# Holding the normalising products of four head pairs back by one pair, and running their reciprocals in one go

## The chip, the cores and the metric

The kernel runs on one NeuronCore of a Trainium2 chip. A core has five engines with a queue of instructions each: TensorE (PE, matmuls; its weight loads are listed apart as PEld), VectorE (DVE), ScalarE (ACT), GpSimd (POOL) and SyncE (SP, which here only issues transfers). Each queue is worked off in its order; an instruction that waits for another engine or for a transfer holds up all that stands behind it in its own queue. Transfers run on 16 DMA engines. The metric is the device time of the launch in microseconds (us); the median of three runs before the change is 471.52 us (471.06 to 471.65).

## The reference

Softmax attention, and on its output a gated feed-forward block (SwiGLU):

```python
# q, k, v: (8, 12, 448, 64)
scores = q @ k.transpose(0, 1, 3, 2) / sqrt(64)
attn = exp(scores - max(scores)); attn = attn / sum(attn)
x = (attn @ v).transpose(0, 2, 1, 3).reshape(3584, 768)
g = x @ w_gate                     # (768, 1536)
out = (silu(g) * (x @ w_val)) @ w_out   # (1536, 768)
```

## The kernel before, in words

**Pairs.** The 96 heads are worked off as 48 pairs; six pairs make a batch of 448 rows, and one X tile holds two batches: pairs 0 to 11 fill the first one. The main loop (L475) has one iteration `pr` for each pair, in which stages of several pairs lie beside one another:

- `load_qk16` (L118) fetches q and k of two pairs ahead, cast to fp16, from POOL's queue; `load_v` (L127) does so for v.
- `prep(pr + 3)` (L497): from pair 11 on, POOL copies q and k into one tile (L156, the two COPY qk<-q and qk<-k), and SP issues a transposing transfer of it (L159). There are three such tiles.
- `qk_half` (L179) makes scores on PE (L186) and their exponentials E on ACT (L193).
- `pv(pr - 1)` (L195): 16 matmuls into the one PSUM bank `acc` (L201), which VectorE copies out to `xr` (L209). There are four xr tiles.
- every other iteration `sums(pr - 2)` (L270) for two pairs: row sums on PE (L224), a copy (`ssb`), and then pieces of work that are put on a list: four reciprocals on VectorE (L278, 112 columns each), and four transfers from SP that spread the result R over partitions as Rb (L285).
- `mult` (L212, L217) multiplies xr by Rb into X on POOL, one instruction for each pair, from pair 6 on. It frees the xr tile and completes X.

**The feed-forward block** is cut in eight blocks of 384 or 512 rows, worked in small steps between the attention stages: gate products (gp) and a tanh on ACT, value products (vp) and two products on VectorE (`ffn1_steps`, L303), then the output products (op), a copy on ACT and the stores from SP (`ffn2_steps`, L335). Block 0 needs pairs 0 to 5 and is added at iteration 6. Block 1 needs pairs 6 to 11 as well and is added at iteration 15; the later ones follow at 21, 27 and so on. The steps of block 0 end with its six output steps, which fall in iterations 11 to 14.

**The order** is written out by hand: each engine gets its instructions as the Python program emits them. Reciprocals, spreading transfers and products are not emitted at once. `sums` puts the four reciprocals and the transfers on the list `deferred`; the products go into `held`, under the iteration at whose end they are moved to `deferred` (L518, L543). `ffn_run` (L461) emits feed-forward steps and after each takes work off `deferred` (L467): one piece after a short step, two after an output step, and the transfers at once when they come to the front. When a block is added, everything deferred is emitted first (L477).

So the iteration under which products are held decides what stands before them in POOL's queue, and the number taken off at a time decides where the reciprocals stand among VectorE's instructions and the transfers among SP's.

Of the kernel before, what the change touches and what calls it, by code (L numbers as in the profile page):

```python
# [27 lines left out]
def kernel(  # L28
# [77 lines left out]
    def dummy(n):  # L106
        wp = ps_f.tile([128, 512], FP32, tag="f", name="wp")
        for _ in range(n):
            nc.tensor.matmul(wp[:], lhsT=warm[:, 0:128], rhs=warm[:], start=True, stop=True)

    def load_qk0():
        rq = raws.tile([P, 2, NC, D], FP32, tag="rq", bufs=RB)
        rk = raws.tile([P, 2, NC, D], FP32, tag="rk", bufs=RB)
        for dst, src in ((rq, q), (rk, k)):
            nc.sync.dma_start(dst[:], src[0, 0:2].rearrange("h (p c) d -> p h (c d)", c=NC))
        raw[0] = (rq[:], rk[:])

    def load_qk16(pr, n=2):  # L118
        q16 = raws.tile([P, 4, NC, D], FP16, tag="rq", bufs=RB, name="q16")
        k16 = raws.tile([P, 4, NC, D], FP16, tag="rk", bufs=RB, name="k16")  # L120
        for dst, src in ((q16, q), (k16, k)):
            flat = src.rearrange("b h s d -> (b h) s d")[2 * pr : 2 * pr + 2 * n]
            nc.gpsimd.dma_start(dst[:, 0 : 2 * n], flat.rearrange("h (p c) d -> p h (c d)", c=NC))
        for i in range(n):
            raw[pr + i] = (q16[:, 2 * i : 2 * i + 2], k16[:, 2 * i : 2 * i + 2])

    def load_v(g, lo=0, hi=2 * GP):  # L127
        b = g // GPB
        h0 = (g % GPB) * 2 * GP
        if lo == 0:  # L130
            v16[g] = raws.tile([P, 2 * GP, NC, D], FP16, tag="vt", bufs=3, name="vt")
        nc.gpsimd.dma_start(
            v16[g][:, lo:hi],
            v[b, h0 + lo : h0 + hi].rearrange("h (p c) d -> p h (c d)", c=NC),
        )
# [247 lines left out]
    with tc.manual_schedule():  # L383
        load_qk0()
        nc.vector.memset(warm[:], 0.0)
        nc.vector.memset(ones[:], 1.0)
        nc.vector.memset(sel[:], 0.0)
        for u in range(2):
            for hx in range(2):
                r = 64 * u + 32 * hx  # L390
                nc.vector.memset(sel[r : r + 1, u, ts(hx, 64)], 1.0)
        load_qk16(1, 1)
        make_identity(nc, ident)
        load_v(0, 0, 2)
        load_qk16(2, 1)
        load_v(0, 2)
        load_qk16(3, 1)
        load_qk16(4)
        load_v(1)
        dummy(7)  # L400
        prep(0)()
        dummy(1)
        turn = prep(1)

        wq = {
            0: [("qk", 6), ("g", 0, 0), ("v", 0, 0)],
            1: [("V", 2), ("qk", 8), ("g", 1, 0), ("v", 1, 0)],
            3: [("g", 2, 0), ("v", 2, 0)],
            4: [("qk", 10), ("g", 2, NCB // 2), ("v", 2, NCB // 2)],
            5: [("V", 3)],  # L410
            6: [("o", 0, 0)],
            7: [("o", 1, 0)],
            8: [("o", 2, 0)],
        }

        def emit(item):
            if item[0] == "qk":
                load_qk16(*item[1:])
            elif item[0] == "V":
                load_v(item[1])  # L420
            else:
                load_w(*item)

        deferred = []
        held = {}
        backlog = []
        state = {"left": 0.0}
        ffn2_wait = []

        def pop_deferred(n=1):  # L430
            for _ in range(n):
                if deferred:
                    deferred.pop(0)()
                while deferred and getattr(deferred[0], "light", False):
                    deferred.pop(0)()

        def add_block(i):
            f1, f2, n = block(i)
            t1, t2 = NCB * n / 2400.0, NFB * OH / 2400.0
            a = [(f1, t1)] * (2 * NFB)  # L440
            pend = list(ffn2_wait)
            ffn2_wait.clear()
            seq = []
            m = len(pend)
            done = 0
            for x in range(len(a)):
                seq.append(a[x])
                want = (x + 1) * m // len(a)
                while done < want:
                    seq.append(pend[done])  # L450
                    done += 1
            seq += pend[done:]
            own = [(f2, t2)] * (2 * (n // 128))
            if i == 0:
                seq += own
            else:
                ffn2_wait.extend(own)
            backlog.extend(seq)
            state["left"] += sum(t for _, t in seq)

        def ffn_run(budget):  # L461
            while backlog and budget > 0:
                gen, t = backlog.pop(0)
                next(gen)
                budget -= t
                state["left"] -= t
                pop_deferred(1 if t < 1.5 else 2)  # L467
            return budget

        carry = 0.0  # L470
        DELAY = 3
        add_at = {FIRST: 0}
        for i in range(1, B - 1):
            add_at[NHP * (i + 1) + DELAY] = i
        for pr in range(NPAIR + 1):  # L475
            if pr in add_at:
                pop_deferred(99)  # L477
            nxt = min([x for x in add_at if x > pr] + [NPAIR + 4])
            slots = 2 * (nxt - pr)
            turn2 = None  # L480
            if pr % 2 == 0 and 12 <= pr + LA < NPAIR:
                load_qk16(pr + LA)
            if pr == NHP:
                pv(pr - 1)
                acc5 = sums64(pr - 1)
                rb4 = scale64(pr - 2, acc4)
                rb5 = scale64(pr - 1, acc5)
                load_table("exp_and_others")
                mult(pr - 2, nc.vector, rb4)
            if pr < NPAIR:  # L490
                qk_half(pr, 0)
            if pr == 0:
                dummy(1)
                turn()
                dummy(1)
            if pr + 3 < NPAIR and pr + 3 >= NPE:
                prep(pr + 3)  # L497
            if pr + 2 < NPAIR:
                if pr + 2 < NPE:
                    turn2 = prep(pr + 2)  # L500
                if (pr + 2) % GP == GP - 1 and 4 <= (pr + 2) // GP + 1 < NGRP:
                    load_v((pr + 2) // GP + 1)
            if pr >= 1 and pr != NHP:
                pv(pr - 1)
            if pr == 5:
                spread23((0,))
            if pr in (2, 4):
                spread = sums_pe(pr - 2, ((0, S),))
            if pr == NHP:
                spread23((1,))  # L510
                mult(pr - 1, nc.vector, rb5)
                dummy(6)
                add_block(0)
                ffn_run(2.5)
            if pr > NHP and pr % 2 == 0:
                work, mults = sums(pr - 2)
                deferred.extend(work)
                held[pr + 1] = mults  # L518
            if pr in add_at and pr != FIRST:
                add_block(add_at[pr])  # L520
            for w in wq.pop(pr, []):
                emit(w)
            tiled[0] = pr >= TILED
            if pr != FIRST:
                carry = ffn_run(state["left"] / slots + carry)
            tiled[0] = False
            if pr < NPAIR:
                qk_half(pr, 1)
            if pr == 0:
                dummy(2)  # L530
            if turn2:
                turn2()
            if pr in (3, 4):
                spread01((pr - 3,))
            if pr == 5:
                acc4 = sums64(pr - 1)
            if pr == 2:
                spread01 = spread
            if pr == 4:
                spread23 = spread  # L540
            if pr == FIRST:
                slots -= 1
            for fn in held.pop(pr, []):  # L543
                deferred.append(fn)
            if not backlog:
                pop_deferred(7)
            carry = ffn_run(state["left"] / max(1, slots - 1) + carry)
        for fns in held.values():
            deferred.extend(fns)
        ffn_run(1e9)  # L550
        pop_deferred(99)
        add_block(B - 1)
        ffn_run(1e9)
        backlog.extend(ffn2_wait)
        ffn_run(1e9)
# [30 lines left out]
```

The softmax here doesn't subtract the row's maximum and nothing guards it: scores larger than these inputs give would overflow.

## Time and profile before

| What | Value |
|---|---|
| time, median of 3 | 471.52 us |
| span of the profiled execution | 470.7 us |
| PE busy | 459.2 us (98%) |
| ACT, DVE, POOL busy | 240.8, 240.7, 146.5 us |
| POOL waiting for Rb (pairs 6 to 47) | 209.2 us in 30 waits |
| PE waiting for X | 3.6 us in 2 waits |
| products of pairs 8 and 9 start | 77.7 and 80.1 us |
| products of pairs 10 and 11 start | 94.65 and 95.7 us |
| block 1's first gate product starts | 91.84 us |
| row sums of pairs 10 and 11 start | 74.63 us |

A timeline row gives the start from the beginning of the span, the length, the engine and line, the operation with the tile written and the tiles read, how many instructions were merged in the row, and in brackets the idle time before it with what ended it. A row of waits gives the total, the number and the longest. A row of windows gives, for a stretch of time, the busy time of PE, PEld, DVE, ACT and POOL, and then PE's granted clock, the DMA share and GB/s.

### The profile page before, as it was taken

The page shows a single profiled execution, that of the slowest core. Times are in us where ns is not written, and L with a number is a line of the kernel's source. Part 1 is how long each engine was busy: PE and PEld are TensorE (multiplying, and loading weights), DVE is VectorE, ACT ScalarE, POOL GpSimd, SP SyncE. Part 2 cuts the span into 40 slices and gives each one's busy share as a digit, 9 for nine tenths or more (in the row PEclk, how much of TensorE's full clock was granted, in tenths as well). Part 3 has the DMA queues.
Part 4 walks back from the last instruction along what each step waited for, and adds up shares of the span by engine and source line. Part 5 has one row for each costly group of instructions (what it writes and reads, how often), then busy time and mean ns, then how long its engine had stood idle before and what let it go on. Part 6 is the DMA issues. An engine that isn't in the chain of part 4 may idle for free.

```text
span 470.7 us, 12521 instructions
## 1 busy us (share of the span) xinstructions
PE 459.2 (98%) x5435; PEld 227.7 (48%) x5435; DVE 240.7 (51%) x375; ACT 240.8 (51%) x350; POOL 146.5 (31%) x200
## 2 busy tenths in 40 slices
PE   8899999879999999999999999999999999999996
PEld 3344444434445555444445555544444555554453
DVE  3665775336764564563654644645636554334310
ACT  4886666636555455455546546546454542222221
POOL 8533352255555225405054054143120011000000
PEclk9999999989999999999999999999999999999999
DMA  9999999999987689647595694884352123201123
GB/s 138 194 203 206 202 191 151 176 167 115 137 138 117 116 138 150 122 50 135 87 142 101 111 154 86 149 105 93 50 115 57 26 68 81 59 1 35 33 68 100
DMA packets 85430, 53.76 MB, mean 114 GB/s; under 512 B 37888, under 2 KB 81920, under 8 KB 85376
## 3 DMA queue, kind: packets, MB, share of 16 engines
q0 software_dynamic: 39200, 23.37, 36.7%
q1 hardware_dynamic: 46112, 29.55, 31.5%
q8 instruction: 42, 0.69, 0.6%
q14 instruction: 12, 0.10, 0.1%
q10 hardware_dynamic: 64, 0.05, 0.0%
HBM read 47.19 MB, written 11.01 MB: 124 GB/s over the span
## 4 chain that ended last, share of the span: by engine, by line
PE 93%; DMA 3%; ACT 1%; POOL 1%; SPq 1%; issue 0%; DVE 0%; POOLq 0%; ACTq 0%
PE op L296 17%; PE vp L296 16%; PE gp L296 12%; PE gp L299 11%; PE s L186 9%; PE vp L299 8%; PE acc L201 8%; PE op L299 5%; PE acc L224 4%; ACT E L193 1%; DMA k<-in_k_dram 1%; DMA Rb<-R 1%; PE rb L263 1%; PE tp L170 1%; SPq L159 0%
## 5 line engine op out<-in xcount | busy, mean ns | idle before, releaser
L193 ACT ACTIVATE E<-s 112x896 f16<-112x896 f32 x192 | 164.6, 915 | 27.6 <-PE s L186 27.5
L217 POOL TENSOR_TENSOR X<-xr,Rb 128x448 f16<-128x448 f32 x42 | 47.7, 1140 | 222.6 <-DMA Rb<-R 209.2
L315 ACT ACTIVATE sg<-gp 128x384 f32<-128x384 f32 (+1 forms) x96 | 52.3, 545 | 100.5 <-PE gp L299 58.5
L327 DVE SCALAR_TENSOR_TENSOR t<-sg,gp 128x384 f32<-128x384 f32 (+1 forms) x96 | 58.8, 612 | 84.7 <-ACT sg L315 84.7
L296 PE MATMUL op<-wo,hts 128*128 128x384 f16 x516 | 89.7, 326 | 0.0
L296 PE MATMUL vp<-X,wv 128*128 128x384 f16 (+1 forms) x378 | 81.6, 352 | 0.0
L330 DVE SCALAR_TENSOR_TENSOR hts<-t,vp 128x384 f16<-128x384 f32 (+1 forms) x96 | 59.6, 621 | 34.2 <-PE vp L296 21.5
L358 ACT ACTIVATE osb<-op 128x384 f32<-128x384 f32 x55 | 27.0, 490 | 95.2 <-PE op L296 67.4
L209 DVE COPY xr<-acc 128x448 f32<-128x448 f32 x48 | 29.8, 621 | 75.6 <-PE acc L201 69.7
L296 PEld LDWEIGHTS <-hts 128*128 128x128 f16 x516 | 49.8, 98 | 37.1 <-issue 2.8
L278 DVE RECIPROCAL R<-ssb 128x112 f32<-128x112 f32 x84 | 66.3, 825 | 0.6
L299 PE MATMUL gp<-X,wg 128*32 128x512 f16 (+1 forms) x1080 | 61.1, 359 | 3.6 <-POOL X L217 3.6
L296 PE MATMUL gp<-X,wg 128*128 128x384 f16 (+1 forms) x306 | 64.6, 348 | 0.0
L186 PE MATMUL s<-qkT 64*128 64x448 f16 x384 | 54.3, 356 | 2.0 <-ACT E L193 1.8
L296 PEld LDWEIGHTS <-wv 128*128 128x128 f16 x378 | 34.9, 98 | 38.1 <-issue 8.2
L201 PE MATMUL acc<-E,vt 112*32 112x448 f16 x768 | 45.2, 355 | 0.0
L299 PE MATMUL vp<-X,wv 128*32 128x512 f16 (+1 forms) x792 | 45.0, 363 | 0.0
L296 PEld LDWEIGHTS <-wg 128*128 128x128 f16 x306 | 28.6, 98 | 28.9 <-issue 6.2
L299 PEld LDWEIGHTS <-wg 128*32 128x32 f16 x1080 | 29.0, 97 | 27.6 <-issue 4.2
L299 PEld LDWEIGHTS <-wv 128*32 128x32 f16 x792 | 21.7, 98 | 17.2 <-issue 0.9
L186 PEld LDWEIGHTS <-qkT 64*128 64x128 f16 x384 | 11.8, 94 | 37.5 <-issue 35.6
L201 PEld LDWEIGHTS <-vt 112*32 112x32 f16 x768 | 16.1, 96 | 25.1 <-issue 16.8
(47 smaller groups left out, 248.0 us busy)
## 6 DMA issues: line engine op xcount, KB each, us to landing
Rb<-R SPq DMA_DIRECT2D x84, 112.0 KB, 2.5
vt<-in_v_dram POOLq DMA_DIRECT2D x15, 336.0 KB, 6.2
q<-in_q_dram POOLq DMA_DIRECT2D x22, 224.0 KB, 4.3
k<-in_k_dram POOLq DMA_DIRECT2D x22, 224.0 KB, 5.7
out_dram<-osb SPq DMA_DIRECT2D x7, 336.0 KB, 3.4
wg<-in_moe_w_gate_dram POOLq DMA_DIRECT2D x4, 576.0 KB, 16.2
wv<-in_moe_w_val_dram POOLq DMA_DIRECT2D x4, 576.0 KB, 17.7
wo<-in_moe_w_out_dram POOLq DMA_DIRECT2D x3, 768.0 KB, 20.0
```

Source lines behind the costliest of these rows:

```text
L186: nc.tensor.matmul(s[:, hx, 0:S], lhsT=t[ts(hx, 64)].rearrange("p c q -> p (c q)")[:, c * P : c * P + 128], rhs=t[ts(hx, 64), NC:, :].rear ...
L193: nc.scalar.activation(E[pr][:, c], s[0:P, :, 0:S], AF.Exp, scale=sm_scale)
L201: nc.tensor.matmul(acc[ts(j, 32), 0:S], lhsT=vt[:, 2 * r + j // 2, c, ts(j % 2, 32)], rhs=E[pr][:, c, j // 2, :], start=(c == 0), stop=(c ...
L209: nc.vector.tensor_copy(xr[:], acc[:, 0:S])
L217: eng.tensor_tensor(X[kk][:, hp, bb * S + lo : bb * S + hi], xraw[pr][:, lo:hi], rb[:, lo:hi], ALU.mult)
L278: work.append(lambda i=i: nc.vector.reciprocal(R[:, ts(i, P)], ssb[:, ts(i, P)]))
L296: nc.tensor.matmul(dst, lhsT=lhsT, rhs=rhs, start=start, stop=stop)
L299: nc.tensor.matmul(dst[ts(j, 32), :], lhsT=lhsT[:, ts(j, 32)], rhs=rhs, start=start, stop=stop)
L315: nc.scalar.activation(sg[:, 0:n], gp[:, 0:n], AF.Tanh, scale=0.5)
L327: nc.vector.scalar_tensor_tensor(t1[:, 0:n], sg[:, 0:n], 1.0, gp[:, 0:n], ALU.add, ALU.mult)
L330: nc.vector.scalar_tensor_tensor(hts[:, fb, 0:n], t1[:, 0:n], 0.5 * HS, vp[:, 0:n], ALU.mult, ALU.mult)
L358: nc.scalar.activation(osb[:, ts(oh, OH)], op[:, 0:OH], AF.Copy, scale=1.0 / HS)
```

## The change

The products of pairs 8 to 11 are held one iteration longer (those of 8 and 9 until iteration 12, those of 10 and 11 until 14), so that loads and copies for later pairs stand ahead of them in POOL's queue. Up to iteration 15, four deferred pieces instead of two are taken off after an output step, so that the four reciprocals of pairs 10 and 11 follow one another and their spreading transfers are emitted sooner.

```diff
-        state = {"left": 0.0}
+        state = {"left": 0.0, "many": 4}
...
-                pop_deferred(1 if t < 1.5 else 2)
+                pop_deferred(1 if t < 1.5 else state["many"])
...
                 work, mults = sums(pr - 2)
                 deferred.extend(work)
-                held[pr + 1] = mults
+                held[pr + (2 if pr in (10, 12) else 1)] = mults
             if pr in add_at and pr != FIRST:
+                state["many"] = 2
                 add_block(add_at[pr])
```

In the built program nothing is added or left out. On POOL the two products of pairs 8 and 9 move behind the q and k loads for pair 18, the copies for pairs 15 and 16 and a load of v; those of pairs 10 and 11 move behind the loads for pair 20 and the copies for pair 17. On VectorE the four reciprocals of pairs 10 and 11 come together, ahead of an xr copy. On SP the four spreading transfers of pairs 10 and 11 move ahead of the transpose of pair 16, and those of pairs 12 and 13 ahead of two output stores.

## Prediction

> **What bounds the kernel now.** I read the page's busy shares first, then what the matmul engine (PE) waited for, then the stretch of its timeline where it waited, then the chain that ended last through that stretch, and last the queue of GpSimd (POOL) before it.
>
> The page, busy shares and granted clock:
>
> ```profile
> PE 459.2 (98%) x5435; PEld 227.7 (48%) x5435; DVE 240.7 (51%) x375; ACT 240.8 (51%) x350; POOL 146.5 (31%) x200
> ...
> PEclk9999999989999999999999999999999999999999
> ```
>
> PE is busy for 98% of the span, the others for half or less. So an edit off PE can gain only where PE stands still, or where its clock is cut. One slice of 40 has a lower clock: the ninth, at 94 to 106 us. The table of waits, for PE alone:
>
> ```profile
> PE gp L299 <- POOL X L217: 3.6, 2, 2.9
> PE s L186 <- ACT E L193: 1.8, 5, 0.4
> ```
>
> The only stall of any size is a gate product that waits for X, twice, 3.6 us. PE's timeline there (start, length, idle before):
>
> ```profile
> 91.84 1.04 PE L299 MATMUL gp<-X,wg 128*32 128x512 f16 x16
> 95.83 0.40 PE L299 MATMUL gp<-X,wg 128*32 128x512 f16 x4 [2.95 <-POOL X L217]
> 96.92 0.46 PE L299 MATMUL gp<-X,wg 128*32 128x512 f16 x4 [0.69 <-POOL X L217]
> 97.13 2.81 PE L299 MATMUL vp<-X,wv 128*32 128x512 f16 x24
> 99.87 0.86 PE L186 MATMUL s<-qkT 64*128 64x448 f16 x4
> ...
> 105.36 1.47 PE L299 MATMUL gp<-X,wg 128*32 128x512 f16 x24
> 106.66 1.47 PE L299 MATMUL vp<-X,wv 128*32 128x512 f16 x24
> ```
>
> This is the first gate product of block 1, in iteration 15. Its first 16 matmuls read pairs 6 to 9; the next four need pair 10 and the last four pair 11. After the gap 24 value matmuls take 2.81 us, where the same 24 take 1.47 at 106.66. The clock in that stretch, by windows of 2 us (the third figure from the end is the share of full speed):
>
> ```profile
> 96.00:98.00 2.00, 1.31 (x17) 0.51 (x16) 0.43 (x1) 0.58 (x1) 2.00 (x3) 0.78 0.00 0
> 98.00:100.00 2.00, 2.00 (x22) 0.69 (x16) 0.71 (x2) 0.02 (x1) 2.00 (x5) 0.50 1.02 123
> ```
>
> 0.78, then 0.50. **What the gap is worth:** from 91.84 to the start of the next gate product at 100.66 it is 8.82 us. The same work (24 gp, 24 vp, 4 s) from 105.36 to 108.55 takes 3.19. The difference is 5.63 us: 3.64 idle, and about 2.0 of slow matmuls.
>
> Why X was late, from the chain that ended last:
>
> ```profile
> 86.29 1.86 SPq L159
> ...
> 88.25 1.18 SPq L285
> ...
> 89.48 5.01 DMA Rb<-R
> ...
> 94.65 0.71 POOL X L217
> ...
> 95.74 1.13 POOL X L217
> ```
>
> The reciprocals of pairs 10 and 11 ended at 81.68 (VectorE's timeline: two at 76.28, two at 80.12), yet their spreading transfers (L285) were issued from 88.25, behind a transpose (L159) and two output stores on SyncE's queue. That queue stood from 73.25 to 83.85 on a transpose whose input POOL had not copied. POOL's timeline says why:
>
> ```profile
> 77.72 1.13 POOL L217 TENSOR_TENSOR X<-xr,Rb 128x448 f16<-128x448 f32 x1 [8.73 <-DMA Rb<-R]
> 80.14 1.13 POOL L217 TENSOR_TENSOR X<-xr,Rb 128x448 f16<-128x448 f32 x1 [1.29 <-DMA Rb<-R]
> ...
> 82.65 0.62 POOL L156 COPY qk<-q 112x512 f16<-112x512 f16 x1
> ```
>
> From 68.99 POOL stood at the products of pairs 8 and 9, whose Rb landed late (7.4 to 8.9 us after issue); the copies for pairs 15 and 16 were queued behind them. So POOL's wait held SyncE, SyncE held Rb of pairs 10 and 11, and that held PE.
>
> **What the Trainium skill says.** "TensorE: Matmul & The Clock Gate", Part 1 (The HAM clock gate): about 3.4 us of idleness halves PE's clock, and as much busy time brings it back; its window runs freely, so the size varies from run to run. The trace agrees: 3.64 us idle, then 0.50 of full clock. "DMA: Bandwidth & Descriptors", Anatomy of one DMA: a wait sits on the issuing sequencer, not in the DMA engines, so what is queued behind it is not even issued; the 6.6 us from 81.68 to 88.25 are that. Same page, Queues, rings and completion order: each DMA engine serves a queue's ring in order and alternates between queues by packets; so more loads in flight slow the Rb transfers. The trace agrees in kind: from 72 to 78 both queues carried packets and Rb took 7.4 to 8.9 us to land, against a median of 2.5 for all 84.
>
> **The change part by part.** No instruction is added or taken away; the built order moves some. (1) On POOL the products of pairs 8 and 9 go behind the loads for pair 18, the copies for 15 and 16 and a load of v. Those of 10 and 11 go behind the load for pair 20 and the copies for 17. (2) On VectorE the four reciprocals of pairs 10 and 11 run in one go, ahead of the xr copy of pair 12. (3) On SyncE the Rb issues of 10 and 11 stand ahead of pair 16's transpose, and those of 12 and 13 ahead of a pair of output stores.
>
> (2) costs nothing: they start at 76.28 and take 2.99 (the row of four at 86.88), so end at 79.27; the xr copy behind them waits for PE until 79.46 anyway. R is ready 2.4 us sooner.
>
> (1) POOL after 68.99: two load issues (0.76 + 0.71), copies for 15 (1.1), v issue (0.77): 72.4. Then the copies for pair 16 wait for their own loads: q, issued at 65.27, landed 11.7 later, at 77.0; k, at 66.02, landed 13.9 later, at 79.9. So they end near 80.5. Rb of 8 and 9 are there by then (77.7, 80.1), so the two products end near 82.8. Here is the added wait: the xr copy of pair 12 (four xraw buffers) needs the product of pair 8 done, near 81.7, and ends at 82.3; PE needs its PSUM bank at 84.47 for the next pv. 2.2 us of slack. Load issues for pair 20 and the copies for 17 follow: 82.8 + 1.45 + 1.1 = 85.4.
>
> (3) SyncE: pair 15's transpose no longer waits (issued by 74.6). Two stores wait for ScalarE's osb, which ends at 78.63; out by 79.7. Then the four Rb issues at 0.6 each: 79.7 to 82.2, where before they ran from 88.25 to 92.40. Their landing is the unknown, as the loads for 18 and v are now in flight with them. Bounds: 3.5 us (shortest here) and 8.9 (the longest on this kernel's Rb rows): 85.1 to 90.5 for the last, issued at 81.6. I take 7.6, the median of the loaded stretch: 89.2. Products of 10 and 11 then end by about 90.4, at the upper bound by 91.6 to 92.8. PE needs pair 10 at 92.7 and pair 11 at 92.9. So X is ready just in time even at the bound.
>
> Sum: 5.63 us come off PE, which is the bound from there to the end (every 10-us window looked at after 100 us shows PE busy throughout). 471.52 - 5.63 = 465.89. I keep 0.1 for waits of a few tenths such as those on E: **466.0**.
>
> **Rivals.**
> - A remnant of the gap. Rb lands later than 8.9 us, since stores of 384 KB and a transpose stand ahead of it in its queue; the transposes of that time took up to 13.1 us to land. At 81.6 + 10.5 = 92.1 the last product ends at 93.3 to 94.4: 0.5 to 1.5 us idle, too short for the clock to drop: 466.5 to 467.4. At 13.1 it is about 3 us, with part of the clock loss: 470. Against it: loads are spread over a stretch with room in it (from 80 to 82 us the DMA share was 0).
> - The wait changes places. The product of pair 8 now stands behind the copies of pair 16, which wait for k. If that lands at 22.1 us (the longest q load of that stretch) rather than 13.9, it is 88.1; pair 8's product ends at 89.9, xr of 12 at 90.5, and PE stands from 84.47 to 90.5. 6.0 us idle plus 2.0 of slow clock, against 5.63 gained, and pair 10's products late on top, some 2 us: 471.5 - 5.6 + 8.0 + 2 = 476. Slower. Against: that 22.1 us load shared the queues with three weight loads, all landed by 71.9.
> - Nothing: Rb is as late as before, because the earlier loads only fill the same DMA engines: 471.5. Against: six us earlier issue is more than any spread of landing here.
>
> **How the numbers follow.** Forecast 0.66; remnant 0.20; wait elsewhere, slower 0.10; nothing 0.04. The range takes the forecast with some 0.8 us below (a different clock loss in other runs) and the remnant up to 3 us: 465.2 to 469.0. It leaves out the last two and the worst remnant, under 2 in 10. Faster 0.87 (forecast, remnant, a little of nothing), same 0.03, slower 0.10.
>
> **What would show it.** Right: PE's waits on X gone or under 1 us, no slice with a lower clock after the start, Rb of 10 and 11 issued near 80, pair 15's transpose issued near 74, pair 16's copies waiting for the k load until about 80, products of 8 and 9 near 81 to 83, of 10 and 11 done before 92.5. Wrong: PE waiting on the xr copy's bank near 84, or still on X near 93; or a gap at a later block's start, which nothing before shows.

## The result, and the profile after

The changed kernel takes 467.15 us (466.85 to 468.27, four runs) against 471.58 for the kernel before (471.06 to 474.2, four runs): a ratio of 0.9899, with a 95% interval of 0.9859 to 0.994. Run again later beside 47 runs of the kernel before it took 467.06 (466.57 to 468.04) against 472.04: 0.9898, 0.9879 to 0.9918. So it is faster by 1.0%, some 4.4 to 5.0 us; the forecast was 466.0.

The page of the changed kernel, busy shares and granted clock:

```profile
PE 457.0 (98%) x5435; PEld 227.3 (49%) x5435; DVE 240.6 (52%) x375; ACT 240.7 (52%) x350; POOL 146.5 (32%) x200
...
PEclk9999999999999999999999999999999999999999
```

It is the same work, and the one slice with a lower clock is gone. In the table of what PE waited for, the longest row is now the one that stood second:

```profile
PE s L186 <- ACT E L193: 1.8, 5, 0.4
```

No row with X is left. PE's timeline at the start of block 1:

```profile
91.17 0.94 PE L201 MATMUL acc<-E,vt 112*32 112x448 f16 x16
91.94 1.47 PE L299 MATMUL gp<-X,wg 128*32 128x512 f16 x24
93.24 1.47 PE L299 MATMUL vp<-X,wv 128*32 128x512 f16 x24
94.64 0.55 PE L186 MATMUL s<-qkT 64*128 64x448 f16 x4
95.12 1.47 PE L296 MATMUL gp<-X,wg 128*128 128x512 f16 x6
```

All 24 gate matmuls come in one row. From 91.94 to the next gate product it takes 3.18 us, where the kernel before took 8.82. That next gate product starts 5.54 us sooner than before, and the span is 5.5 us shorter, so in these two executions the whole gain arises here. GpSimd's timeline, with what it waited for in brackets:

```profile
77.37 0.61 POOL L156 COPY qk<-q 112x512 f16<-112x512 f16 x1 [4.68 <-DMA q<-in_q_dram]
80.77 0.61 POOL L156 COPY qk<-k 112x512 f16<-112x512 f16 x1 [2.79 <-DMA k<-in_k_dram]
81.35 2.23 POOL L217 TENSOR_TENSOR X<-xr,Rb 128x448 f16<-128x448 f32 x2
...
88.78 2.22 POOL L217 TENSOR_TENSOR X<-xr,Rb 128x448 f16<-128x448 f32 x2 [2.66 <-DMA Rb<-R]
```

The copies of pair 16 now wait for their own loads ahead of the products of pairs 8 and 9; those of pairs 10 and 11 end at 91.0 instead of 96.9. SyncE's queue in the kernel before, where the row of two transposes stretched to 85 us:

```profile
71.79 13.29 SPq L159 DMA_TRANSPOSE qkT<-qk  x2
...
88.25 4.15 SPq L285 DMA_DIRECT2D Rb<-R  x4
```

and in the changed kernel:

```profile
71.99 6.24 SPq L159 DMA_TRANSPOSE qkT<-qk  x2
...
79.77 2.40 SPq L285 DMA_DIRECT2D Rb<-R  x4
```

The row of transposes now ends at 78.2, and Rb of pairs 10 and 11 is issued 8.5 us sooner. Some 2.6 us of this are lost again, because these four transfers now land 8.1 to 8.5 us after their issue, where it was 3.5 to 5.8 before; the products end 5.9 us sooner. The price is in VectorE's timeline:

```profile
82.52 0.62 DVE L209 COPY xr<-acc 128x448 f32<-128x448 f32 x1 [3.16 <-POOL X L217]
```

The xr copy of pair 12 waits for the product of pair 8. It ends at 83.1, and PE uses the freed bank at 84.57, so this wait is hidden.

### The profile page after: what moved, and what is told of

Read it like the earlier page. It is cut to its first block, busy times and chain, and to the rows that moved or that the text cites. A ratio compares the mean times of both kernels' runs of the same rounds, so it can differ in the third digit from the quotient of the medians.

```text
span 465.2 us, 12522 instructions
## 1 busy us (share of the span) xinstructions
PE 457.0 (98%) x5435; PEld 227.3 (49%) x5435; DVE 240.6 (52%) x375; ACT 240.7 (52%) x350; POOL 146.5 (32%) x200
## 4 chain that ended last, share of the span: by engine, by line
PE 95%; DMA 2%; ACT 1%; POOL 1%; issue 0%; DVE 0%; ACTq 0%; POOLq 0%
PE op L296 18%; PE vp L296 16%; PE gp L296 12%; PE gp L299 11%; PE s L186 9%; PE acc L201 9%; PE vp L299 8%; PE op L299 5%; PE acc L224 4%; ACT E L193 1%; DMA k<-in_k_dram 1%; PE rb L263 1%; PE tp L170 1%; DMA out_dram<-osb 0%; PE acc L236 0%
## 5 line engine op out<-in xcount | busy, mean ns | idle before, releaser
L299 PE MATMUL vp<-X,wv 128*32 128x512 f16 (+1 forms) x792 | 43.7, 355 | 0.0
```

The lines of the kernel that those rows point to most:

```text
L299: nc.tensor.matmul(dst[ts(j, 32), :], lhsT=lhsT[:, ts(j, 32)], rhs=rhs, start=start, stop=stop)
```

## Experiments

The theory was a chain of queues: GpSimd's wait for Rb of pairs 8 and 9 held the copies of pair 15, these held SyncE's queue, that held Rb of pairs 10 and 11, and that PE. The rivals were that the reciprocals alone were late, or that transfers were slow wherever they stood. In some runs of the kernel before PE's clock was cut and in others it was not, so the mean granted clock of each run is used beside its time. The runs with the hold alone, the reciprocals alone, the filled gap and the changed kernel ran on one chip, beside 47 runs of the kernel before (median 472.04); the second profile of the hold alone and the last three experiments ran on another, beside 30 (median 471.56).

**The longer hold alone** (against the changed kernel):

```diff
-        state = {"left": 0.0, "many": 4}
+        state = {"left": 0.0, "many": 2}
```

> The longer hold alone, with two pieces of deferred work after an output step as before. Queue theory (GpSimd's wait held SyncE's queue, which held Rb of pairs 10 and 11): pair 15's transpose is issued near 74 us, but the second two reciprocals of pairs 10 and 11 now stand behind the xr copy that waits for the product of pair 8, so R is done only near 84.7 and Rb is issued near 85 to 87, landing 92 to 94; a gap of 1 to 2.5 us on PE near 93 remains: 468 to 469.5 us. Rival, hold alone suffices: no wait on X, as the changed kernel, 467. Rival, the reciprocals in one go are the whole effect: 471.5.

Measured: 471.24 us, ratio 0.9981 (0.9966 to 0.9996), 22 runs. VectorE, SyncE, GpSimd and PE in the profiled run:

```profile
82.10 0.62 DVE L209 COPY xr<-acc 128x448 f32<-128x448 f32 x1 [4.59 <-POOL X L217]
82.64 1.55 DVE L278 RECIPROCAL R<-ssb 128x112 f32<-128x112 f32 x2
```

```profile
84.22 2.41 SPq L285 DMA_DIRECT2D Rb<-R  x4
```

```profile
93.25 2.22 POOL L217 TENSOR_TENSOR X<-xr,Rb 128x448 f16<-128x448 f32 x2 [7.53 <-DMA Rb<-R]
```

```profile
94.43 0.40 PE L299 MATMUL gp<-X,wg 128*32 128x512 f16 x4 [1.87 <-POOL X L217]
95.52 0.40 PE L299 MATMUL gp<-X,wg 128*32 128x512 f16 x4 [0.69 <-POOL X L217]
```

The steps came as expected: the hold made two of the reciprocals stand behind the very copy that waits for the held product, so R was done at 84.2, later than in the kernel before (81.7). The time did not: only 4 of the 22 runs, the profiled one (469.44) among them, lie in the expected 468 to 469.5. Nine runs with a clock of 0.998 or more have a median of 469.65, thirteen with 0.996 or less one of 471.76. To see the other kind, the same kernel was profiled once more.

> The longer hold alone once more, for its profile: 13 of its 22 runs had a mean clock of 0.996 or less and a median of 471.8 us, the other 9 one of 469.7. Theory that a stall of PE near the length at which the clock halves decides between them: a run of the slow kind shows a halved clock at 96 to 100 us and a somewhat longer wait for X; one of the fast kind (as the one profiled) 1.9 and 0.7 us of wait and the full clock. Rival, the waits for X alone differ by 2 us between runs, with the clock cut elsewhere.

This execution was of the other kind, and further out: it took 472.79 us with a mean clock of 0.992, where the lowest of the 22 runs is 0.994. PE's timeline and the windows after it (third figure from the end: the granted clock):

```profile
95.24 0.62 PE L299 MATMUL gp<-X,wg 128*32 128x512 f16 x4 [2.42 <-POOL X L217]
96.33 0.62 PE L299 MATMUL gp<-X,wg 128*32 128x512 f16 x4 [0.47 <-POOL X L217]
96.70 2.80 PE L299 MATMUL vp<-X,wv 128*32 128x512 f16 x24
```

```profile
96.00:98.00 2.00, 1.67 (x17) 0.70 (x20) 0.38 (x1) 0.60 (x1) 2.00 (x4) 0.50 1.10 370
98.00:100.00 2.00, 2.00 (x20) 0.48 (x12) 0.76 (x2) 0.00 (x0) 1.24 (x2) 0.50 1.78 170
```

The waits are longer by 0.3 us in all (2.89 against 2.56; the first alone 2.42 against 1.87), and the clock is halved, so the difference between the two kinds is not one of the waits alone. In the medians it is 2.1 us. One execution of each kind does not show whether the length of the wait decided or the moment at which it fell.

**The reciprocals in one go alone** (against the changed kernel):

```diff
-                held[pr + (2 if pr in (10, 12) else 1)] = mults
+                held[pr + 1] = mults
```

> The reciprocals in one go alone, products held as before. Queue theory: the copies of pairs 15 and 16 still stand behind the products of pairs 8 and 9, so SyncE stands until near 84; but Rb of pairs 10 and 11 now goes ahead of pair 16's transpose, near 86.2 to 88.6 instead of 88.25 to 92.4, and lands at 91 to 93; a gap of 1 to 2 us remains: 468 to 470 us. Rival, the reciprocals are the whole effect: 467. Rival, they are nothing, since R was ready long before: 471.5.

Measured: 469.74 us, ratio 0.9955 (0.994 to 0.997). SyncE and PE:

```profile
72.26 13.07 SPq L159 DMA_TRANSPOSE qkT<-qk  x2
...
86.56 4.23 SPq L285 DMA_DIRECT2D Rb<-R  x4
```

```profile
91.75 0.55 PE L186 MATMUL s<-qkT 64*128 64x448 f16 x4 [1.12 <-DMA qkT<-qk]
...
94.93 0.40 PE L299 MATMUL gp<-X,wg 128*32 128x512 f16 x4 [0.90 <-POOL X L217]
```

As the queue theory said: SyncE still stands until 85, Rb starts only 1.7 us sooner than before, and a wait for X remains (0.90, and 0.69 for pair 11). The row above it shows a second wait: PE stood 1.12 us for pair 15's transposed tile, whose copy stood behind the products of pairs 8 and 9. In one of ten runs the mean clock was below 0.996. The hold alone brings 0.8 us, the reciprocals alone 2.3, both together 5.0, more than the sum: neither alone makes the gain.

**The gap filled** (against the kernel before):

```diff
+            if pr == 15:
+                dummy(14)
             if pr in add_at and pr != FIRST:
                 add_block(add_at[pr])
```

> The kernel before, with 14 matmuls of zeros (0.21 us each, 3.0 us) ahead of block 1's first gate product, so that PE works while X is on its way; nothing is left out of the result. Theory that 5.6 us of loss were 3.6 us of idleness and 2.0 us of a halved clock: the idleness stays (filled or not), the slow matmuls after it go, no window below 0.9 of full clock: 469.5 us. Rival, the slow matmuls come from something else than the idleness, such as the transfers: 471.5, with slow matmuls still there at 97 to 100 us.

Measured: 471.0 us, ratio 0.998 (0.997 to 0.9989), 22 runs, all with a clock of 0.998 or more. PE's timeline:

```profile
91.84 0.55 PE L186 MATMUL s<-qkT 64*128 64x448 f16 x4 [1.43 <-DMA qkT<-qk]
...
93.20 3.19 PE L109 MATMUL wp<-warm 128*128 128x512 f16 x14
96.32 1.48 PE L299 MATMUL gp<-X,wg 128*32 128x512 f16 x24
97.63 1.47 PE L299 MATMUL vp<-X,wv 128*32 128x512 f16 x24
```

The mechanism holds: with PE at work while X was on its way the matmuls after it take 1.47, not 2.81, though X came no sooner. The size was off (469.5 expected). The reason is in the runs of the kernel before: 33 of its 47 runs beside these have a mean clock of 0.996 or less, median 472.19; the other 14 have 0.998 or more, median 470.85. Filling the gap turned all runs into those of full clock, and gained their difference for the share of runs that had it to lose: 1.34 x 33/47 = 0.94, measured 1.04.

**The changed kernel again.**

> The changed kernel once more, for the size: the forecast of 5.6 us less rests on the gap of one profiled execution of the kernel before. If the gap is as long in its other executions: 5.5 us less than before, span of 465.2. If it is shorter or varies there, some 4 to 5 us, with spans of the kernel before that spread by 1 us or more and those of this kernel by less.

Measured: 467.06 us, spans from 464.8 to 466.3; all ten runs of this kernel have a clock of 0.998 or more. The second reading came true: before the change 47 runs spread by 3.5 us (470.19 to 473.72), after it ten by 1.7; the 14 runs before with a clock of 0.998 or more spread by 1.5.

**Rb from ScalarE's queue** (against the kernel before):

```diff
-                    nc.sync.dma_start(rv[w], R[ts(u, 64), :])
+                    (nc.scalar if p0 == 10 else nc.sync).dma_start(rv[w], R[ts(u, 64), :])
```

> The kernel before, with the four Rb transfers of pairs 10 and 11 alone issued from ScalarE's queue; GpSimd's order, the reciprocals and everything else as before. Queue theory: the only thing between R (81.7 us) and X was SyncE's queue, so Rb is issued near 82 to 84.5, lands by 88 to 91, and PE no longer waits for X; ScalarE pays for the issues, about 2.4 us ahead of the next exponentials, of which PE sees 1 to 2 us near 84 to 86: 468 to 469.5 us, no halved clock. Rival, the transfers themselves were slow in the busy DMA engines, whatever their place in a queue: X as late as before, 471 to 472.

Measured: 469.55 us, ratio 0.995 (0.9931 to 0.997). ScalarE's issues, GpSimd, PE:

```profile
81.61 2.45 ACTq L285 DMA_DIRECT2D Rb<-R  x4
```

```profile
86.28 1.14 POOL L217 TENSOR_TENSOR X<-xr,Rb 128x448 f16<-128x448 f32 x1 [0.23 <-DMA Rb<-R]
89.45 1.14 POOL L217 TENSOR_TENSOR X<-xr,Rb 128x448 f16<-128x448 f32 x1 [2.03 <-DMA Rb<-R]
```

```profile
85.08 0.37 PE L186 MATMUL s<-qkT 64*128 64x448 f16 x2 [1.16 <-ACT E L193]
85.89 0.36 PE L186 MATMUL s<-qkT 64*128 64x448 f16 x2 [0.44 <-ACT E L193]
...
93.41 0.55 PE L186 MATMUL s<-qkT 64*128 64x448 f16 x4 [1.04 <-DMA qkT<-qk]
...
94.66 1.47 PE L299 MATMUL gp<-X,wg 128*32 128x512 f16 x24
```

This separates the theories most sharply. GpSimd's order and the reciprocals are those of the kernel before; only the queue from which four transfers are issued differs, and X is ready at 90.6. The transfers landed 2.3 to 6.1 us after their issue, against 3.5 to 5.8 in the kernel before. So SyncE's queue was the link, not slow transfers. What it costs shows too: 1.60 us for the exponentials behind the issues, and again about 1 us for pair 15's tile.

**The hold of pairs 8 and 9 longer still** (against the changed kernel, held until iteration 14):

```diff
-                held[pr + (2 if pr in (10, 12) else 1)] = mults
+                held.setdefault(pr + {10: 4, 12: 2}.get(pr, 1), []).extend(mults)
```

> The changed kernel with the products of pairs 8 and 9 held two iterations more, behind the loads for pair 20 and the copies of pair 17 as well; it adds 2.6 us to the wait of the xr copy of pair 12. Theory of the slack: that copy then ends near 86 instead of 82.5, while PE wants its bank at 84.57, so PE stands about 1.5 us there, and X is still ready in time (near 91.5): 468.3 to 468.8 us. Rival, the wait has more slack than 2 us, or another buffer frees PE: 467. Rival, the delay adds up and X is late too: 470 or more.

Measured: 470.87 us, ratio 0.9984 (0.9972 to 0.9997), 22 runs. VectorE, PE, and the windows:

```profile
86.23 0.62 DVE L209 COPY xr<-acc 128x448 f32<-128x448 f32 x1 [7.22 <-POOL X L217]
```

```profile
86.91 0.94 PE L201 MATMUL acc<-E,vt 112*32 112x448 f16 x16 [2.49 <-DVE xr L209]
...
88.99 3.25 PE L299 MATMUL op<-wo,hts 128*32 128x384 f16 x48
```

```profile
88.00:90.00 2.00, 2.00 (x31) 1.10 (x27) 1.27 (x3) 0.00 (x0) 0.64 (x1) 0.50 1.32 242
```

The place was right, the size was not: 2.49 us instead of 1.5 (the copies of pair 17 waited 1.33 us for a tile to come free), and that again halved the clock; 17 of the 22 runs have a mean clock of 0.996 or less. X was in time. One more step of the hold gives back nearly all of the gain.

**The hold of pairs 10 and 11 as before** (against the changed kernel):

```diff
-                held[pr + (2 if pr in (10, 12) else 1)] = mults
+                held[pr + (2 if pr == 10 else 1)] = mults
```

> The changed kernel without the longer hold of pairs 10 and 11: their products now follow those of 8 and 9 at once and wait there for Rb, with the loads for pair 20 and the copies of pair 17 behind them. Theory: Rb lands near 88 in either order, so X is ready as soon, and the copies of pair 17, near 91 to 93 then, are needed only near 105: 467 us, this part of the change is worth nothing. Rival, GpSimd standing once more holds SyncE's queue (pair 17's transpose, then Rb of pairs 12 and 13) and brings a wait back: 468 or more.

Measured: 467.16 us, ratio 0.9908 (0.989 to 0.9927). GpSimd and SyncE:

```profile
88.01 2.22 POOL L217 TENSOR_TENSOR X<-xr,Rb 128x448 f16<-128x448 f32 x2 [5.18 <-DMA Rb<-R]
```

```profile
92.81 1.22 SPq L159 DMA_TRANSPOSE qkT<-qk  x1
94.13 3.22 SPq L285 DMA_DIRECT2D Rb<-R  x4
```

GpSimd stands longer, SyncE issues Rb of pairs 12 and 13 4 us later than in the changed kernel (94.13 against 89.99), and PE waits for no X in this profile. The changed kernel itself did not run on this chip; its ratio on the other one, 0.9898 (0.9879 to 0.9918), overlaps with this one. So no gain from this part of the change shows.

## Why the prediction was right, and where its size was off

- **What bounds the kernel** and the chain behind the one wait: right, and shown, by the changed kernel and by the run with ScalarE's queue.
- **What the gap is worth**, 5.63 us: right for the execution it was read from. The span of the profiled one went from 470.7 to 465.2, 5.5 less.
- **The sum, 471.52 - 5.63**: this is the mis-sized term. It took the loss of one execution, with a halved clock, off a median over executions that did not all have it. The profiled one took 472.47 us; less 5.63 that is 466.84, and the changed kernel's profiled run took 466.94. Over many runs those with a cut clock are 1.34 us longer, and they are 33 of 47, or 0.9 us on average, where the working took 2.0 for all; the idle part is 470.85 - 467.06 = 3.8, where it took 3.64. Together that is 4.7; the medians give 5.0 and 4.4. The share varies: on the other chip the clock was cut in 17 of 30 runs, with 1.30 us between the medians.
- **Reciprocals in one go "costs nothing"**: right (the xr copy behind them waited for the product of pair 8 in any case), but their use was undersold as "2.4 us sooner". With two pieces taken off at a time the hold puts two of them behind the added wait, and most of the gain is lost.
- **GpSimd's order**: copies of pair 16 to end near 80.5, measured 81.4; products to end near 82.8, measured 83.6; slack of the xr copy 2.2 us, measured 1.4.
- **SyncE and the landing of Rb**: issues forecast for 79.7 to 82.2, measured 79.77 to 82.17, but partly by luck. Pair 15's transpose, forecast to be out by 74.6, was out only at 78.2, because its issue alone took 4.66 us (1.23 in the kernel before); the stores behind it waited for ScalarE until 78.7 in any case, so 0.4 us of room was left in this profile. Why the issue took so long these runs don't show. Landing was taken as 7.6 us and measured 8.1 to 8.5, near the upper bound of 8.9. Products of pairs 10 and 11 forecast to end by 90.4, measured 91.0, about 1.9 us ahead of their use.
- **The rival in which the wait changes places** had a sound mechanism: the run with the longer hold shows it at the place named. In the changed kernel k landed near 80.7, not 88.
- **What was missed**: pair 15's transposed tile. Its transpose was issued at 83.85 in the kernel before and landed 6.5 us later, at 90.4, and PE began to use the tile at 90.6: no wait of note in that profile. In the three profiles with the reciprocals alone, the filled gap and ScalarE's queue, which all leave these copies behind the products, it was issued at 84.1 to 84.3, landed 7.6 to 9.2 us later, and cost PE 1.0 to 1.4 us. In the run with the filled gap the added matmuls come only after this wait, so other executions of the kernel before probably have it too; no second profile of that kernel shows it. The hold removes it: in the changed kernel the transpose was issued at 73.57 and landed 13.2 us later, at 86.8, where PE wants the tile at 90.7. Advancing Rb alone leaves it, as the run with ScalarE's queue shows.

## What to carry to other kernels

When an engine's only stall is at the end of a chain of queues, look for the first wait in the chain and ask what is queued behind it: moving the waiting instruction back behind independent work can gain what no faster instruction would. Check what else then stands behind the moved one; here the hold needed the reciprocals to be taken out of its shadow. And take a loss read from one execution off the time of that execution, not off a median, above all when a clock state is part of it.

## What the hardware showed beyond what was expected

"TensorE: Matmul & The Clock Gate", Part 1, puts the idleness that halves PE's clock at about 3.4 us. Here less was enough. With one wait of 2.49 us (the longer hold) 17 of 22 runs had a mean clock of 0.996 or less, and with 1.87 or 2.42 us and a shorter wait after it (the hold alone) 13 of 22. With 1.12, 0.90 and 0.69 us in the profiled run (the reciprocals alone) it was 1 of 10 runs, with 1.16, 0.44 and 1.04 (ScalarE's queue) none of 9, so waits of about 1 us were mostly, but not always, too short. Among the longer waits no order by length shows: the kernel before, with 2.95 and 0.69, had 33 of 47 and 17 of 30.

Windows of half a microsecond show when the clock fell: in the kernel before, in the run with the longer hold, and in the second profile of the hold alone.

```profile
97.00:97.50 0.50, 0.50 (x8) 0.22 (x11) 0.00 (x0) 0.08 (x1) 0.50 (x1) 0.62 0.00 0
```

```profile
87.50:88.00 0.50, 0.50 (x16) 0.34 (x12) 0.03 (x1) 0.00 (x0) 0.00 (x0) 0.82 1.23 289
```

```profile
94.50:95.00 0.50, 0.00 (x0) 0.00 (x0) 0.00 (x0) 0.00 (x0) 0.50 (x1) 0.87 3.22 110
```

Worked out from these means, the clock fell near 97.1, 87.8 and 94.9 us: 1.3 us after the long wait was over, 0.9 us after it, and 0.4 us before its end. Half clock lasted 3.4 us in the first two and 6.8 us in the third, by the windows in which it came back. At half clock 3.4 us hold 1.7 us less of matmul work, an estimate from these windows; the working took 2.0, and the medians of the kernel before show 1.34. The page says that its window runs freely, and a fall at no fixed distance from the wait agrees with that. At which length of wait the fall becomes certain these runs don't show.
